# New places in the instruction order of all five engines, in a kernel of attention with a Hyena gate

## The chip, the cores and the metric

The kernel runs on one core of one Trainium2 chip. The metric is the device time of one execution in microseconds (us); it is given as the median of several runs. A core has five instruction queues that matter here: PE (TensorE, the matmuls), ACT (ScalarE), DVE (VectorE), POOL (GpSimd) and SP (SyncE, which here only issues DMA transfers). Each works through its own queue strictly in order.

## What is computed

For each of 8 batches, 12 heads attend over 448 positions of 64 values. The denominator of the softmax has one more term, as if there were one more key with score 0. The heads of a position side by side make the 768 columns of `x`, which goes through a projection, a convolution along the sequence (by Fourier transform, with one filter for each column), a gate and an output projection.

```python
scores = scale * np.matmul(q, k.transpose(0, 1, 3, 2))
m = np.max(scores, axis=-1, keepdims=True)
e = np.exp(scores - m)
attn = e / (np.sum(e, axis=-1, keepdims=True) + np.exp(-m) + 1e-09)
x = heads_side_by_side(np.matmul(attn, v))           # 8 x 448 x 768
proj = x @ w_proj                                    # 768 x 2304
x1, x2, x3 = proj[..., :D], proj[..., D:2*D], proj[..., 2*D:]
x2_conv = np.fft.irfft(np.fft.rfft(x2, n=S, axis=1) * H, n=S, axis=1)
y = x1 * x2_conv * x3
out = y @ w_out                                      # 768 x 768
```

## The kernel before

**Tiling.** Two heads make a pair; a batch has 6 pairs, the whole input 48, numbered `i` (pair 12 is the first of batch 2, the third batch). For each pair TensorE computes the transposed scores (`scores`, L835 to L842) in four tiles of keys, `t` = 0 to 3: three of 128 keys, and tile 0 with the last 64 keys of both heads. ScalarE takes the exponential (L844), TensorE multiplies with V, which has a column of ones for the denominator (`out_rests` L867, `out_rest` L876 with the matmul at L879), and VectorE normalises into `xb` (L887). Then `xb` is turned to `xT`, by TensorE or by a DMA transpose.

**How Q and K are turned.** Batches 0 and 1 are "staged" (`staged`, L449): SP loads q, k and v of a pair (the tasks `sq`, `sk`, `sv`; 224, 192 and 192 KB), POOL or VectorE casts them to bf16 (`cq`, `ck`, `cv`; casts of v at L505), and TensorE turns q and k (`T`). From batch 2 on (`loaded`, L592) POOL casts likewise, and then SP issues DMA transposes from `qn` to `qT` (L600) and from `kn` to `kT` (L607), one pair at first and three at a time later. The transpose of K of pair 12 (`kT12`) needs the cast `ck12`, the two casts `crk2` of the batch's last 64 keys (L621, from the load `rk2`) and the memset of `kn` (`zero kn`, L1507). The first scores of a pair, S(i,0), need its `kT` and `qT`.

**Dense part of a batch** (`dense`, L1012). The projection to x2 is done in the folded domain of the transform (`proj2`, L1065 to L1068, with weights `w(1,0)` and `w(1,1)`, or `still2` for later batches, with DMA transposes between), then the products with the filter's spectrum (`product`, L1154), the two gates (`gate`, L1187, with weights `w(0)` and `w(2)`), the inverse transform, the gating, and the projection by `w_out` (`output`, L1000), whose tiles ScalarE copies out and SP stores. The weights are loaded and cast to bf16 by DMAs that POOL issues: `filt`, `w(0)`, `w(1,0)`, `w(1,1)`, `w(2)` (`wproj_load`, L816 to L818) and `wout` (L822 to L823, 1152 KB in bf16). While batch b is in its dense part, the attention of batch b + 1 runs on the same engines; the instructions are interleaved.

**What sets the order.** The kernel's body doesn't write the instructions out in sequence. Each piece of work is handed to a planner as a task (`add`, L77): an engine, a cost, what it needs and makes, and which ring buffers it takes and gives back. There are 2027 tasks: 605 on PE, 549 on DVE, 453 on ACT, 243 on SP, 177 on POOL. The planner sorts each engine's tasks and plays the program through with the costs, to place tiles in PSUM banks and to put idle matmuls into gaps of the first 36 us. Where the list `ORDER` is set (L406), the k-th task's number in it is the key by which its engine's tasks are sorted, and the engine takes only the first of its queue:

```python
want = self.ORDER[len(self.tasks)] if self.ORDER else want + self.SHIFT.get(part, 0.0)
queue = {e: sorted(t for t in self.tasks if t[2] == e) for e in self.LAT}
for i, t in enumerate(queue[e][: 1 if self.ORDER else self.WINDOW]):
```

So an engine's instructions run in the order of these numbers, whatever the costs say, and an instruction that waits for data holds up all behind it on its engine. SP's queue holds loads, DMA transposes and stores in one sequence.

Of the kernel before, what the change touches and what calls it, by code (L numbers as in the profile page):

```python
# [300 lines left out]
def kernel(  # L301
# [92 lines left out]
    def stage(g, at, n):  # L394
# [4 lines left out]
    plan = Plan(  # L399
        {  # L400
            "e": 6, "er": 2, "k0": 2, "q0": 2, "u": 1, "w": 1, "xf": 1,
            "x2": 1, "x2s": 1, "x2h": 1, "xs": 2, "t0": 2, "t1": 2, "yh": 1, "g": 1, "x1": 2, "cr": 2, "cw": 1, "cv": 2, "yT": 1, "yR": 1,
            "os": 3,
        }
    )
# [1126 lines left out]
    with (  # L1532
# [6 lines left out]
        for b in range(n_batches):  # L1539
            W["yT", b], W["yR", b // 2] = y, yr  # L1540
            stable(b)
            plan = Plan(plan.size)
# [9 lines left out]
    with tc.manual_schedule(engines={E.PE, E.Pool, E.DVE, E.Activation, E.SP}):  # L1552
        plan = main
# [31 lines left out]
```

## Time and profile before

| | before |
|---|---|
| median of 3 runs | 376.19 us |
| lowest and highest run | 375.47, 376.73 us |
| span of the profiled execution | 375.5 us |
| ScalarE, VectorE, GpSimd busy | 264.3, 259.1, 114.7 us |
| TensorE busy | 361.1 us |

The profile is of one execution. A line of a table of groups gives engine, operation, tile and source line; in the timeline the first two numbers are the start and the duration, and a bracket at the end is the idle time just before with what ended it. SP's queue is shown as SPq and POOL's as POOLq. A DMA issue's line belongs to the helper that issues it: L601 for the transposes to `qT`, L608 for those to `kT`, L818 for `w`, L823 for `wout`. A transfer's "us to landing" runs from its issue to its last byte. A table of windows gives, for a stretch of time, each engine's busy time with the number of instructions, then the granted clock of TensorE (1.00 is full), the share of the DMA engines and GB/s.

### The profile page before, as it was taken

To read this page: it belongs to the slowest core of one execution; us is meant where nothing else is said; L and a number is where in the kernel's file an instruction comes from. 1 tells how busy PE (TensorE), PEld (TensorE's weight loads), DVE (VectorE), ACT (ScalarE), POOL (GpSimd) and SP (SyncE) were. 2 spreads that over 40 slices of the span, in tenths; PEclk is the share of its full clock that TensorE was granted. 3 is DMA by queue.
4 is the path that set the end of the run, shared out by engine and by line. 5 is a ranking of instruction groups with operands and counts; after the bars stand their busy time and mean duration, and the time that the engine had idled before them with its cause. 6 is when DMAs were issued, how large, how long until landed. Compare 5 with 4: busy or idle time off the path is not lost. (4 is left out here: it accounts for less than half of the span.)

```text
span 375.5 us, 9312 instructions
## 1 busy us (share of the span) xinstructions
PE 361.1 (96%) x3596; PEld 216.8 (58%) x3596; DVE 259.1 (69%) x676; ACT 264.3 (70%) x455; POOL 114.7 (31%) x240
## 2 busy tenths in 40 slices
PE   7999999799999999999899999999999999999995
PEld 6656665446755576655456556655555556555653
DVE  7589479845699657895299938685467855958770
ACT  4988976657886767788379568877788776536533
POOL 5862818024435363473264415330000000000000
PEclk9999999989999999999999999999999999999999
DMA  8999999999998999999999999787273026343214
GB/s 220 258 248 231 252 223 210 131 234 249 225 243 209 223 290 204 281 229 218 239 244 199 275 206 205 218 160 177 58 114 86 2 41 170 44 112 58 88 44 170
DMA packets 132018, 68.40 MB, mean 182 GB/s; under 512 B 88765, under 2 KB 128384, under 8 KB 131968
## 3 DMA queue, kind: packets, MB, share of 16 engines
q1 hardware_dynamic: 127248, 62.11, 73.5%
q0 software_dynamic: 4480, 5.41, 9.0%
q8 instruction: 29, 0.48, 0.5%
q10 hardware_dynamic: 240, 0.23, 0.2%
q14 instruction: 21, 0.17, 0.2%
HBM read 43.86 MB, written 11.01 MB: 146 GB/s over the span
## 5 line engine op out<-in xcount | busy, mean ns | idle before, releaser
L853 ACT ACTIVATE e<-psum 128x896 bf16<-128x896 f32 x144 | 126.8, 921 | 25.4 <-PE psum L840 21.2
L1190 PE MATMUL psum<-xT,wproj_bf 128*128 128x448 bf16 x576 | 122.1, 352 | 0.3 <-DVE ldm L1101 0.2
L1190 PEld LDWEIGHTS <-wproj_bf 128*128 128x128 bf16 x576 | 53.8, 97 | 46.1 <-issue 2.7
L1004 PE MATMUL psum<-wout_bf,yT 128*128 128x384 bf16 x288 | 53.9, 331 | 0.7 <-DVE g L1205 0.6
L879 PE MATMUL psum<-vn,e 128*128 128x65 bf16 x1152 | 47.5, 194 | 0.0
L879 PEld LDWEIGHTS <-e 128*128 128x128 bf16 x1152 | 41.6, 98 | 5.2 <-issue 0.8
L840 PE MATMUL psum<-qT,kT 64*128 64x448 bf16 x288 | 41.4, 357 | 0.3 <-ACT e L853 0.2
L637 POOL CAST nat<-nat 112x512 bf16<-112x512 f32 x36 | 26.0, 728 | 46.2 <-DMA nat<-in_q_dram 42.0
L1158 DVE TENSOR_TENSOR t<-xs,hrs 113x768 bf16<-113x768 bf16 (+1 forms) x64 | 37.3, 607 | 3.1 <-ACT xs L1152 2.7
L1004 PEld LDWEIGHTS <-yT 128*128 128x128 bf16 x288 | 27.3, 99 | 20.9 <-issue 3.9
L1090 PE MATMUL psum<-xf,wproj_bf 128*128 128x452 bf16 x180 | 38.8, 357 | 0.0
L1311 ACT COPY osb<-psum 128x384 f32<-128x384 f32 x56 | 25.7, 486 | 18.4 <-PE psum L1004 11.2
L859 ACT ACTIVATE er<-psum 128x448 bf16<-128x448 f32 x48 | 26.4, 552 | 17.1 <-PE psum L842 16.2
L1205 DVE TENSOR_TENSOR g<-x,psum 128x448 bf16<-128x448 bf16 x48 | 29.4, 615 | 12.2 <-PE psum L1190 8.5
L1152 ACT CAST xs<-psum 113x384 bf16<-113x384 f32 (+1 forms) x64 | 28.7, 486 | 9.5 <-PE psum L1140 5.7
L894 DVE TENSOR_TENSOR xb<-psum,den 128x512 bf16<-128x512 f32 x48 | 33.2, 691 | 1.7
L1245 ACT CAST cr<-psum 128x452 bf16<-128x452 f32 x48 | 24.7, 546 | 11.2 <-PE psum L1236 10.0
L1202 ACT CAST x<-psum 128x448 bf16<-128x448 f32 x48 | 25.6, 537 | 8.3 <-PE psum L1190 6.0
L892 DVE TENSOR_SCALAR den<-psum 128x8 f32<-128x8 f32 x48 | 7.9, 164 | 34.0 <-PE psum L879 32.7
L669 POOL CAST vn<-nat 128x192 bf16<-128x192 f32 x58 | 22.2, 409 | 21.4 <-DMA nat<-in_v_dram 16.9
L1068 PE MATMUL psum<-wproj_bf,xf 128*113 128x384 bf16 x144 | 27.0, 328 | 0.7 <-DMA wproj_bf<-in_moe_w_proj_dram 0.7
L657 POOL CAST nat<-nat 128x384 bf16<-128x384 f32 x29 | 18.0, 623 | 29.4 <-DMA nat<-in_k_dram 24.0
(128 smaller groups left out, 460.1 us busy)
## 6 DMA issues: line engine op xcount, KB each, us to landing
nat<-in_q_dram SPq DMA_DIRECT2D x47, 224.0 KB, 4.2
out_dram<-osb SPq DMA_DIRECT2D x24, 384.0 KB, 3.6
nat<-in_k_dram SPq DMA_DIRECT2D x41, 192.0 KB, 4.4
nat<-in_v_dram SPq DMA_DIRECT2D x41, 192.0 KB, 4.7
wproj_bf<-in_moe_w_proj_dram POOLq DMA_DIRECT2D x2, 1152.0 KB, 14.7
rests<-in_k_dram SPq DMA_DIRECT2D x8, 192.0 KB, 4.3
rests<-in_v_dram SPq DMA_DIRECT2D x8, 192.0 KB, 4.2
out_dram<-osb SPq DMA_DIRECT2D x8, 192.0 KB, 3.2
```

What stands on the lines that cost most here:

```text
L840: nc.tensor.matmul(sc[:, u, 0:S], kT[b % 2][c, hp, t, :], qT[b % 2][c, hp, :])
L853: nc.scalar.activation(to, of, AF.Exp, scale=SCALE)
L859: nc.scalar.activation(to, of, AF.Exp, scale=SCALE)
L879: nc.tensor.matmul(out_bank(u)[:, n, :], P["e"][1 + t][:, u * S + n * 128 : u * S + n * 128 + 128], vn[b % 2][:, hp, 4 * u + t, :], start= ...
L894: nc.vector.tensor_tensor(W["xb", b][:, hp].rearrange("p n (u d) -> p u n d", u=2), op[:, :, :, 0:DH], rec[:].unsqueeze(3).to_broadcast([1 ...
L1004: nc.tensor.matmul(ops[:n, :DCH], y[:, dt, 0:n], wout_bf[:, dt, ch * DCH : (ch + 1) * DCH], start=(dt == 0), stop=(dt == NDT - 1),)
L1068: nc.tensor.matmul(pps[:FQ, :DCH], W["xf", b][:, pg, kt, 0:FQ], wproj_bf[:, kt, D + ch * DCH : D + (ch + 1) * DCH], start=(kt == 0), stop= ...
L1090: nc.tensor.matmul(pps, wproj_bf[:, kt, D + dt * 128 : D + (dt + 1) * 128], W["xf", b][:, :, kt, 0:FQ], start=(kt == 0), stop=(kt == NDT - 1),
L1152: nc.scalar.copy(L["xs", par, ch][:K, pg % 2, :], L["Z", pg, ch][:K, :DCH])
L1158: nc.vector.tensor_tensor(t[:K], L["xs", par, ch][:K], h, op=ALU.mult)
L1190: nc.tensor.matmul(p[:, :S], wproj_bf[:, kt, 2 * part * D + dt * 128 : 2 * part * D + (dt + 1) * 128], xT()[:, kt, 0:S], start=(kt == 0), ...
L1205: nc.vector.tensor_tensor(g[:, dt, :], L["x1", dt], p[:, :S], op=ALU.mult)
```

## The change

One line differs, L406: the list `ORDER` has 2027 new numbers.

```diff
-    plan.ORDER = (17, 4, 0, 94, 7, 9, 8, 11, 21, 19, 26, 30, 5, 12, 200, 3, 6, 23, 2, 18, 13, 14,
+    plan.ORDER = (2, 2, 3, 171, 0, 3, 1, 0, 4, 1, 2, 3, 11, 1, 0, 0, 1, 6, 0, 5, 5, 9, 8, 7, 5,
...
```

Before, the numbers are one ranking of all tasks, from 0 to 2026; after, they count within each engine. Since only the order within an engine is read, what matters is a task's place in its engine's queue. No task, cost, tile, buffer or instruction is added or taken away. The place is the same as before for 186 of 605 tasks on PE, 156 of 453 on ACT, 91 of 549 on DVE, 34 of 243 on SP and 16 of 177 on POOL. A task moves by 1.6 places on PE, 1.3 on ACT, 3.0 on DVE, 4.4 on POOL and 4.6 on SP in the mean, and by at most 16 on PE, 46 on SP and 155 on POOL. The moves that matter below:

| queue | task | place before | place after |
|---|---|---|---|
| POOL | first DMA of 32 bytes (L1463; nobody waits for it) | 16 | 171 |
| POOL | `pads` (zeros in the exponentials' tiles) | 2 | 11 |
| POOL | `crv0` (cast of the last keys' V, batch 0) | 8 | 13 |
| POOL | load `filt` | 9 | 15 |
| POOL | loads `w(0)`, `w(1,0)` | 20, 21 | 21, 27 |
| POOL | load `w(1,1)` | 36 | 33 (behind `cv6`, ahead of `ck8`, `cq8`) |
| POOL | load `w(2)` | 38 | 38 |
| POOL | load `wout` | 54 | 42 (behind `cq10`, ahead of `cv7`, `ck11`, `cv8`, `cq11`) |
| POOL | casts `crk2`; `ck12` | 50, 55; 58 | 51, 53; 52 |
| SP | loads `sv7`, `sv8` | 24, 35 | 33, 36 |
| SP | loads `sq11`, `sk11` | 37, 38 | 34, 35 |
| SP | transposes `qT12`, `kT12` | 50, 52 | 46, 49 |
| SP | loads `sv13`, `sq15`; transpose `qT13` | 45, 49; 51 | 51, 56; 53 |
| SP | a store of batch 2 | 189 | 173 |
| SP | x2 transpose of batch 3; an xT transpose | 160; 103 | 152; 99 |
| DVE | memset `zero kn` | 74 | 91 |
| PE | S(12,0) | 131 | 131 |

In SP's queue after, the places 26 to 36 hold `sk8`, `sq8`, `sk9`, `sq9`, `sk10`, `sq10`, `sv9`, `sv7`, `sq11`, `sk11` and `sv8`, in this order. On PE, five output tiles of the last batch come in another sequence; their stores don't.

2 lines of the change are left out of this document (1 added, 1 removed).

## The prediction

> **What bounds the kernel now.** I read the page's head and clock row first, then the table of waits of TensorE, then the windows around its longest wait.
>
> ```profile
> span 375.5 us, 9312 instructions
> PE 361.1 (96%) x3596; PEld 216.8 (58%) x3596; DVE 259.1 (69%) x676; ACT 264.3 (70%) x455; POOL 114.7 (31%) x240
> PEclk9999999989999999999999999999999999999999
> ```
>
> TensorE is busy for 361.1 of 375.5 us, and the next engine for 264.3. So the time is TensorE's work plus what it waits for; an order can change only the second, some 14 us, and what the clock loses. The clock row has one 8, in its ninth slice (75 to 84 us). The profiled execution's span is 375.5 us and the median 376.19; I work on the span and add the 0.7 at the end.
>
> ```profile
> PE psum L842 <- DMA kT<-nat: 3.2, 1, 3.2
> PE psum L1480 <- DVE idle L1468: 2.0, 1, 2.0
> PE psum L1140 <- DMA x<-ldm: 0.8, 1, 0.8
> PE psum L1068 <- DMA wproj_bf<-in_moe_w_proj_dram: 0.7, 2, 0.5
> PE psum L842 <- DVE xT L985: 0.7, 1, 0.7
> ```
>
> The columns are the total, the count and the longest. The longest wait by far is at L842, the first scores of pair 12, for pair 12's DMA transpose of K. L1480 is the start of the program.
>
> ```profile
> 72.00:74.00 2.00, 0.76 (x5) 0.20 (x2) 2.00 (x6) 0.63 (x2) 0.00 (x0) 1.00 1.41 137
> 74.00:76.00 2.00, 0.06 (x1) 0.06 (x1) 0.55 (x2) 0.00 (x0) 0.00 (x0) 1.00 1.15 165
> 76.00:78.00 2.00, 2.00 (x39) 1.39 (x40) 0.12 (x1) 1.66 (x3) 0.80 (x2) 0.89 1.16 306
> 78.00:80.00 2.00, 2.00 (x8) 0.86 (x6) 1.87 (x6) 0.50 (x1) 0.92 (x3) 0.50 1.24 257
> 80.00:82.00 2.00, 2.00 (x12) 0.70 (x11) 1.77 (x5) 0.92 (x1) 0.00 (x0) 0.76 1.57 174
> ```
>
> After the length of the window come PE, PEld, DVE, ACT, POOL, then the granted clock, the DMA share and GB/s. TensorE all but stops from 72.8 to 75.9, and behind that the clock falls to 0.89, 0.50 and 0.76. TensorE is full there, so the loss is 0.22 + 1.00 + 0.48 = 1.7 us. One late transpose costs 3.2 + 1.7 = 4.9 us.
>
> Why it was late, from the timeline and the DMA issues (the first three from 60.2 to 66 us, the last two of the whole run; KB each, then us to landing):
>
> ```profile
> 60.32 0.82 POOL L823 DMA_DIRECT2D wout_bf<-in_moe_w_out_dram  x1
> ...
> 63.52 0.85 DVE L1158 TENSOR_TENSOR t<-xs,hrs 112x768 bf16<-112x768 bf16 x1
> 64.14 3.92 SPq L608 DMA_TRANSPOSE kT<-nat  x1
> 70.33 2.43 PE L1190 MATMUL psum<-xT,wproj_bf 128*128 128x448 bf16 x12
> 75.94 0.36 PE L842 MATMUL psum<-qT,kT 128*128 128x448 bf16 x1 [3.18 <-DMA kT<-nat]
> ```
>
> ```profile
> wout_bf<-in_moe_w_out_dram POOLq DMA_DIRECT2D x1, 1152.0 KB, 14.1
> qT<-nat SPq DMA_TRANSPOSE x2, 13.2
> kT<-nat SPq DMA_TRANSPOSE x1, 11.8
> ```
>
> ```profile
> qT<-nat SPq DMA_TRANSPOSE x16, 4.5
> kT<-nat SPq DMA_TRANSPOSE x16, 4.4
> ```
>
> The load of the output weights was issued at 60.32, the transposes right behind it, and they took 11.8 to 13.2 us where the median of the run is 4.4. The transpose of K was issued at 64.14, landed at 75.9, and was needed at 70.33 + 2.43 = 72.8.
>
> **The change part by part.** Nothing is added or removed: no instruction, tile or wait on a semaphore, only places in the queues. So each cost is a wait that goes or comes.
>
> *Output weights ahead (POOL place 54 to 42).* They are now issued right behind cq10 and w(2), some 10 us earlier, and are through when the transposes come.
>
> ```profile
> DMA packets 2330, 1.79 MB, mean 149 GB/s; under 512 B 1252, under 2 KB 2328, under 8 KB 2328
> q0 software_dynamic: 783, 1.18, 78.3%
> q1 hardware_dynamic: 1545, 0.59, 39.6%
> ```
>
> ```profile
> DMA packets 1420, 1.61 MB, mean 230 GB/s; under 512 B 45, under 2 KB 1419, under 8 KB 1419
> ...
> q1 hardware_dynamic: 694, 0.57, 31.6%
> ```
>
> The first fence is 62 to 74 us (q0 is GpSimd's queue, q1 SyncE's; packets, MB, share): load and transposes together moved 149 GB/s. The second is 24 to 31 us, a weight load beside plain loads: 230 GB/s. At about 226, the 1.79 MB of 62 to 74 take 7.9 us instead of 12: 4.1 earlier. In SyncE's queue sv13, sq15 and qT13 (0.42 MB) also move behind K's transpose: 0.42 / 0.23 = 1.8 us. The transpose then lands at 75.9 - 5.9 = 70.0.
>
> Its issue is gated too: it needs the memset of kn (L1507), which moves back from place 74 to 91 on VectorE, where the work stood at 63.52 (row above), and behind it on POOL two casts of the shared rows and ck12, 0.5 us each:
>
> ```profile
> 53.34 0.38 DVE L1507 MEMSET nat<- 128x384 uint32 x1
> 61.19 0.51 POOL L621 CAST nat<-rests 64x384 bf16<-64x384 f32 x1
> ```
>
> The memset thus ends at about 64.4 at the latest, the three casts at 65.9, the issue is at 66.2, and with the median 4.4 us it lands at 70.6. Both ways leave 2 us before 72.8. Wait **-3.2**, clock **-1.7**. Bounds: nothing gained at one end, -4.9 at the other; I take the far end because both estimates have slack.
>
> *w(1,1) ahead (POOL place 36 to 33: behind cv6, ahead of ck8 and cq8).*
>
> ```profile
> 34.04 0.64 POOL L505 CAST vn<-nat 128x192 bf16<-128x192 f32 x2 [1.06 <-DMA nat<-in_v_dram]
> 38.41 0.82 POOL L818 DMA_DIRECT2D wproj_bf<-in_moe_w_proj_dram  x1
> ```
>
> ```profile
> 48.70 1.18 PE L1068 MATMUL psum<-wproj_bf,xf 128*113 128x384 bf16 x6 [0.52 <-DMA wproj_bf<-in_moe_w_proj_dram]
> 54.16 0.93 PE L879 MATMUL psum<-vn,e 128*128 128x65 bf16 x24
> ```
>
> It was issued at 38.41 and is now issued at 34.7, when cv6 ends, so the 0.52 us at 48.70 goes: **-0.5**.
>
> *What it meets: V of pair 8.* The same load now runs beside SyncE's loads of pairs 8 to 11, and in SyncE's queue V of pair 8 stands at 36, behind sk8, sq8, sk9, sq9, sk10, sq10, sv9, sv7, sq11 and sk11. These and itself are 7 x 0.197 + 4 x 0.229 = 2.29 MB. Its cast cv8 releases the output matmuls of pair 8 (L879, at 54.16; TensorE would be there at 53.7 with the 0.5 gained). SyncE's rate, from 37 to 42 us without a weight load and from 43 to 48 and 49 to 55 with one, and last GpSimd's queue from 38 to 43:
>
> ```profile
> DMA packets 1611, 1.27 MB, mean 255 GB/s; under 512 B 98, under 2 KB 1611, under 8 KB 1611
> ```
>
> ```profile
> q0 software_dynamic: 774, 0.66, 81.6%
> q1 hardware_dynamic: 649, 0.48, 39.0%
> ```
>
> ```profile
> q1 hardware_dynamic: 1411, 0.46, 38.0%
> ```
>
> ```profile
> q0 software_dynamic: 106, 0.08, 10.4%
> ```
>
> Alone 255 GB/s; beside w(1,1) 0.48 MB in 5 us, 96 GB/s; beside w(2) 0.46 in 6 us, 77 (and by the fence of 24 to 31, 0.57 in 7, 81). By 36.4, when the load before it, w(1,0), is through, I count 0.16 MB of the 2.29 as done (an estimate, most of one transfer). From there: w(1,1)'s bytes start at about 38.7, 4 us behind its issue (issued at 38.41, its queue had moved only 0.08 MB by 43), 2.3 us at 255 = 0.59 MB; w(1,1) takes 0.59 MB / 0.132 = 4.4 us, 0.42 MB beside it; about 1.1 us until w(2) starts, 0.28 MB. There remain 0.84 MB beside w(2) at 81: 10.4 us, until 54.6. With the cast (0.64) cv8 is there at 55.3, against 53.7 to 54.2: a wait of 1.1 to 1.6. I take **+1.3**. Bounds: 0, if w(2) starts later; 7.9, worked out below.
>
> *The first 36 us* (filter 9 to 15, pads 2 to 11, crv0 8 to 13 on POOL). ScalarE sets the pace there:
>
> ```profile
> 10.00:20.00 10.00, 9.58 (x143) 6.24 (x143) 5.43 (x17) 9.65 (x15) 8.96 (x19) 1.00 1.14 252
> ```
>
> ScalarE is busy for 9.65 of 10 us, and its order hardly moves. I take 0, with the waits below 1 us of the table as bounds, about 2 either way.
>
> *After 85 us* SyncE's order (store(2,2) 189 to 173, some x transposes up to 8 places earlier) can move the waits of L1140 and L842: -1.5 (0.8 + 0.7) if both go, +4.9 if a transpose meets a load as in 64 to 76. I take 0: no weight load is left there, the first DMA (POOL 16 to 171) has nobody waiting for it, and TensorE's own moves (16 places at most) keep the work the same around each wait above. *Tail*: the last batch's output tiles are computed in another sequence and stored in the same one; 0 to +0.3, taken as 0.
>
> Sum: -3.2 - 1.7 - 0.5 + 1.3 = -4.1 us; span 371.4, and by the median 376.19 - 4.1 = **372.1 us**.
>
> **Rivals.**
>
> *V of pair 8 becomes the late transfer (slower).* Beside back-to-back weight loads SyncE moved only 0.59 MB in 12 us (49 GB/s) from 62 to 74. If it gets no more behind w(1,1), with w(2) and the output weights now following each other, the 0.84 MB take 17.1 us, to 61.3; cv8 comes at 62.0, a wait of 7.9, and a wait this long halves the clock too, 1.7. That is -5.4 + 7.9 + 1.7 = +4.2: 380.4. It decides from a wait of 3.7, which is 65 GB/s. For it: the three loads stand closer together than before. Against it: those 12 us held transposes, and without them SyncE had 77 to 96 beside a load. 0.15; 0.05 more for a like delay elsewhere.
>
> *K's transpose stays late.* The load may not have slowed it; then only the 1.8 us of moved items come off, it lands at 74.1, 1.3 are left of the wait, the clock stays full: -1.9 - 1.7 - 0.5 + 1.3 = -2.8, 373.4. Against it: 13.2 and 11.8 us beside the load, 4.4 in the median. 0.11. [...] The trace's 149 against 230 GB/s speaks against it.
>
> *Given back later.* A transpose or a store behind 85 us is delayed, 2.3 us of wait and 1.7 of clock: 376.1, no change. For it: SyncE's later places move most (46 at most). Against it: every wait there is below 1 us. 0.13.
>
> *All goes well.* V of pair 8 is in time (-1.3) and the 0.8 and 0.7 go as well: 369.3. 0.08.
>
> [...]
>
> **How the numbers follow.** The forecast (370.5 to 373.5) has 0.48, the others 0.15 + 0.05, 0.11, 0.13, 0.08. The range goes from the last rival to a V wait halfway into the first: 369.2 to 378.0. About 0.3%, 1.1 us, is what a measurement can tell from no change: faster 0.48 + 0.11 + 0.08 = 0.67, same 0.13, slower 0.20.
>
> **What would show it.** The output weights issued near 50; K's transpose of pair 12 landed in under 7 us, before 72; no L842 row of 3.2; no 8 in the clock row's ninth slice; no wait at L1068 at 48; a wait of about 1 us at L879 near 54 for pair 8's cast. Wrong if that wait is above 3.7 us, if K's transpose is still the late one, or if waits below 36 or beyond 85 us change by more than 1 us.

## The result, and the profile after

| | before | after |
|---|---|---|
| median of 20 runs each | 376.40 us | 379.31 us |
| lowest and highest | 372.74, 381.06 | 377.20, 382.30 |
| ratio, with 95% interval | | 1.0106 (1.0078 to 1.0133) |
| span of the profiled execution | 375.5 us | 377.0 us |

The changed kernel is slower, by 1.06% or 4.0 us. The ratio is taken from the executions in the faster of two states, which leaves out the dearest of the kernel before; over all 20 of each the medians differ by 2.9 us. Forecast was 372.1, and 379.31 lies above the range that was given (369.2 to 378.0). First the head of the page of the changed kernel:

```profile
span 377.0 us, 9293 instructions
PE 359.6 (95%) x3584; PEld 216.1 (57%) x3584; DVE 255.8 (68%) x676; ACT 263.4 (70%) x455; POOL 109.4 (29%) x240
PEclk9999999999999999999999999999999999999998
```

The 8 in the ninth slice is gone (the one in the last slice lies behind the last matmul). TensorE is busy for 359.6 instead of 361.1 us, nearly the 1.7 us that the clock cost (twelve idle matmuls fewer are in it too). So the part of the prediction that it was about came true, and yet the span is longer. TensorE's waits in the changed kernel (total, count, longest):

```profile
PE psum L1190 <- DMA wproj_bf<-in_moe_w_proj_dram: 1.5, 1, 1.5
PE psum L1140 <- DMA x<-nat: 1.4, 1, 1.4
PE psum L840 <- DVE xb L894: 1.4, 1, 1.4
PE psum L1068 <- DMA wproj_bf<-in_moe_w_proj_dram: 1.2, 1, 1.2
...
PE psum L840 <- DVE g L1205: 0.7, 1, 0.7
```

The row of L842 with its 3.2 us is gone. In its place stand rows of 0.7 to 1.5 us, at several places of the kernel; five of them are shown. From the timeline and the DMA issues (66 to 70 us) of the changed kernel, the chain that was mended:

```profile
42.89 0.82 POOL L823 DMA_DIRECT2D wout_bf<-in_moe_w_out_dram  x1
62.96 1.32 SPq L601 DMA_TRANSPOSE qT<-nat  x1
66.93 3.55 SPq L608 DMA_TRANSPOSE kT<-nat  x2
```

```profile
kT<-nat SPq DMA_TRANSPOSE x2, 3.3
```

Pair 12's transpose of K was issued at 66.93 (66.2 was predicted) and landed at 71.0, before TensorE needed it.

**Where the time goes.** The order of TensorE's work differs, so I compare by work done: for each point, the time at which TensorE had done so much, less the streaming time of that work at full clock (the same in every column, so it cancels in the differences). The growth of this number in a stretch is what TensorE lost there, waits and half clock together, in us. The times of the heads are those of the changed kernel. Two further profiles of the kernel before (e5 and e6, below) and two of the changed one with small edits (e4, e10) show how much of it is one execution's chance. The profile of e10 is of its dearest execution (379.43 us, the others 375.6 to 377.6):

| stretch | before: first, e5, e6 | after, e4, e10 | difference of the means |
|---|---|---|---|
| 2 to 71 us | 18.5, 18.2, 18.2 | 19.2, 20.5, 19.2 | +1.3 |
| 71 to 109 | 7.2, 4.8, 5.8 | 3.0, 2.2, 2.9 | -3.2 |
| 109 to 187 | 6.4, 6.1, 5.7 | 7.9, 7.0, 8.6 | +1.7 |
| 187 to 272 | 4.7, 4.6, 4.6 | 5.6, 6.1, 7.9 | +1.9 |
| 272 to 279 | 0.4, 0.4, 0.4 | 2.0, 1.1 (e10 mends it: 0.5) | +1.1 |
| 279 to 368 | 3.9, 3.9, 3.9 | 4.1, 4.1, 4.0 | +0.1 |
| last matmul to the end | 4.2 | 5.3 (e4 mends it: 4.2) | +1.1 |

The sum is +4.0 us, of which 0.2 go off because TensorE starts that much earlier; the measured ratio is 4.0 us. The stretch that the prediction was about gained 3.2 us; all the others lost 7.2.

**The end** is the plainest of them. The last issues on SyncE's queue, the changed kernel first and then the kernel before, each with the last store's KB and us to landing:

```profile
371.61 1.11 SPq L1321 DMA_DIRECT2D out_dram<-osb  x2
372.82 0.54 SPq L1318 DMA_DIRECT2D out_dram<-osb  x1
...
out_dram<-osb SPq DMA_DIRECT2D x1, 384.0 KB, 3.3
```

```profile
370.24 1.14 SPq L1321 DMA_DIRECT2D out_dram<-osb  x2
372.19 0.34 SPq L1318 DMA_DIRECT2D out_dram<-osb  x1
...
out_dram<-osb SPq DMA_DIRECT2D x1, 384.0 KB, 2.3
```

With the new sequence of tiles the issue of tile 3's two stores ends only 0.1 us ahead of the last store's, instead of 0.8. Beside them the last store took 3.3 instead of 2.3 us.

### The profile page after: what moved, and what is told of

The parts are those of the page before. It is cut to its first block, busy times and chain, and to the rows that moved or that the text cites. A ratio compares the mean times of both kernels' runs of the same rounds, so it can differ in the third digit from the quotient of the medians.

```text
span 377.0 us, 9293 instructions
## 1 busy us (share of the span) xinstructions
PE 359.6 (95%) x3584; PEld 216.1 (57%) x3584; DVE 255.8 (68%) x676; ACT 263.4 (70%) x455; POOL 109.4 (29%) x240
## 5 line engine op out<-in xcount | busy, mean ns | idle before, releaser
L1190 PEld LDWEIGHTS <-wproj_bf 128*128 128x128 bf16 x576 | 53.5, 97 | 47.2 <-issue 3.1
L1004 PE MATMUL psum<-wout_bf,yT 128*128 128x384 bf16 x288 | 52.9, 326 | 0.4 <-DVE g L1205 0.4
L879 PEld LDWEIGHTS <-e 128*128 128x128 bf16 x1152 | 42.8, 98 | 5.7 <-issue 0.8
L637 POOL CAST nat<-nat 112x512 bf16<-112x512 f32 x36 | 23.5, 655 | 72.2 <-DMA nat<-in_q_dram 38.0
L840 PE MATMUL psum<-qT,kT 64*128 64x448 bf16 x288 | 41.3, 355 | 2.5 <-DVE xb L894 1.4
L1158 DVE TENSOR_TENSOR t<-xs,hrs 113x768 bf16<-113x768 bf16 (+1 forms) x64 | 36.4, 592 | 3.1 <-ACT xs L1152 3.0
L1068 PE MATMUL psum<-wproj_bf,xf 128*113 128x384 bf16 x144 | 26.4, 328 | 1.2 <-DMA wproj_bf<-in_moe_w_proj_dram 1.2
L669 POOL CAST vn<-nat 128x192 bf16<-128x192 f32 x58 | 21.1, 394 | 20.0 <-DMA nat<-in_v_dram 18.9
L1090 PEld LDWEIGHTS <-wproj_bf 128*128 128x128 bf16 x180 | 16.4, 96 | 16.8 <-issue 1.5
```

The source lines that it names most:

```text
L840: nc.tensor.matmul(sc[:, u, 0:S], kT[b % 2][c, hp, t, :], qT[b % 2][c, hp, :])
L879: nc.tensor.matmul(out_bank(u)[:, n, :], P["e"][1 + t][:, u * S + n * 128 : u * S + n * 128 + 128], vn[b % 2][:, hp, 4 * u + t, :], start= ...
L1004: nc.tensor.matmul(ops[:n, :DCH], y[:, dt, 0:n], wout_bf[:, dt, ch * DCH : (ch + 1) * DCH], start=(dt == 0), stop=(dt == NDT - 1),)
L1068: nc.tensor.matmul(pps[:FQ, :DCH], W["xf", b][:, pg, kt, 0:FQ], wproj_bf[:, kt, D + ch * DCH : D + (ch + 1) * DCH], start=(kt == 0), stop= ...
L1090: nc.tensor.matmul(pps, wproj_bf[:, kt, D + dt * 128 : D + (dt + 1) * 128], W["xf", b][:, :, kt, 0:FQ], start=(kt == 0), stop=(kt == NDT - 1),
L1158: nc.vector.tensor_tensor(t[:K], L["xs", par, ch][:K], h, op=ALU.mult)
```

## The experiments

**Halves and single moves (e1 to e4).** Theory: the early part of the new order gains, the late part gives back. The rivals said that the gain was chance, or that the loss was early. All four ran on one chip against the same runs of before (375.59 us).

```diff
 e1, POOL's queue of before, one load moved:
   ... cq10,
+  wout,
   ck10, cv11, cv9, cv8, cv10, cq11, ck11, crk2, crv2, cq13, cq12,
-  wout,
   crk2, cv13, ck14, ck12 ...
 e2: all five queues new for what starts before 85 us, then before's order
 e3: before's order for what starts before 85 us, then the new one
 e4, the changed kernel, TensorE's last tiles as in before:
-  (3,1) (2,0) (1,1) (3,0) (2,1)
+  (1,1) (3,0) (3,1) (2,1) (2,0)
```

> Before's order with one task moved: the output weights' load goes from place 54 to 42 of POOL's queue, as in the changed kernel. Theory (the wait of pair 12 for its transpose of K costs 4.9 us in every execution, and the load is its cause): that wait and the half clock behind it go, ratio to before 0.987 to 0.990. Rival 1 (the load is the cause, but the profiled execution of before had an unusually long wait, and the typical one loses less): the profile shows the early load and no wait, ratio 0.994 to 1.000. Rival 2 (the load isn't the cause, or its new place delays SyncE's loads as much): a wait of over 2 us at pair 8 or 12 in the profile, ratio 1.000 or above.

> All engines in the new order for what starts in the first 85 us, in before's order from there. Theory (the new order gains early and gives it back late): by the profiles TensorE is 4.0 to 4.4 us ahead of before at 85 us, ratio 0.988 to 0.991. Rival 1 (the early gain is a matter of the one profiled execution of before): 0.996 to 1.002. Rival 2 (the loss is early, in the waits for the weights at 33 and 38 us): 1.004 or above.

> All engines in before's order for what starts in the first 85 us, in the new order from there. Theory (the loss is late: by the profiles 4.8 us of new waits between 90 us and the last matmul and 0.9 in the last stores): ratio 1.012 to 1.016. Rival 1 (the late waits are chance, the loss is early): 0.998 to 1.002. Rival 2 (part of the late loss only follows from TensorE being early, so that it isn't there when the early part is late): 1.003 to 1.008.

> The changed kernel, with the last batch's output tiles and their copies in before's sequence. Theory (with the new sequence two stores of tile 3 are issued right ahead of the last store, which then takes 4.2 instead of 3.3 us to land): 0.9 us less than the changed kernel, ratio to before 1.007 to 1.009. Rival (the end's difference between the two profiles is chance): as the changed kernel, 1.0106, within its interval of 1.008 to 1.013.

| run | median | ratio to before | 95% interval |
|---|---|---|---|
| e1, the load alone | 377.70 us | 1.0067 | 1.0029 to 1.0105 |
| e2, early part new | 379.01 | 1.0094 | 1.0059 to 1.0128 |
| e3, late part new | 379.90 | 1.0137 | 1.0072 to 1.0203 |
| e4, new with old tail | 378.31 | 1.0066 | 1.0030 to 1.0102 |

e3 is as the theory had it: the late part of the new order costs 1.4% by itself. e4 is in its direction, 0.4% below the changed kernel (the intervals overlap; that the end is mended is read from its trace, 4.2 us from the last matmul as in before). e1 and e2 refute the theory's other half: both take away the wait at pair 12 and are slower than before (e1 has the ratio of its second rival without its wait). In e1 only one load is moved. Its DMA queues from 50 to 60 us, and below them those of e5 (the kernel before) in the same stretch; q0 is GpSimd's weight loads, q1 SyncE's transfers:

```profile
q0 software_dynamic: 1074, 1.61, 87.9%
q1 hardware_dynamic: 1393, 0.48, 27.1%
```

```profile
q1 hardware_dynamic: 3266, 1.66, 89.9%
q0 software_dynamic: 410, 0.61, 33.1%
```

SyncE's queue moved 0.48 MB in these 10 us instead of 1.66 (the changed kernel: 0.53). The delay didn't go; it moved from pair 12's transposes to the loads of pairs 12 to 15: in e1 the Q load of pair 12 landed at 63.96 instead of 59.51. GpSimd's casts of these loads came later with it, and met other work of VectorE. VectorE in e1, with what it ran beside on GpSimd, and then e5:

```profile
69.29 0.38 DVE L1256 TENSOR_TENSOR cw<-cr 128x444 bf16<-128x444 bf16 x1
69.59 0.88 DVE L1254 TENSOR_TENSOR cw<-cr 128x452 bf16<-128x452 bf16 x1
70.50 1.31 DVE L1265 TENSOR_TENSOR cv<-cw 128x448 bf16<-128x448 bf16 x2
```

```profile
69.55 0.61 POOL L637 CAST nat<-nat 112x512 bf16<-112x512 f32 x1 [2.56 <-DMA nat<-in_q_dram]
70.11 0.85 POOL L669 CAST vn<-nat 128x192 bf16<-128x192 f32 x2
70.91 0.66 POOL L657 CAST nat<-nat 128x384 bf16<-128x384 f32 x1
```

```profile
69.65 0.39 DVE L1256 TENSOR_TENSOR cw<-cr 128x444 bf16<-128x444 bf16 x1
69.95 0.40 DVE L1254 TENSOR_TENSOR cw<-cr 128x452 bf16<-128x452 bf16 x1
70.38 0.69 DVE L1265 TENSOR_TENSOR cv<-cw 128x448 bf16<-128x448 bf16 x2
```

The same three instructions take 0.88 and 1.31 us beside the casts and 0.40 and 0.69 without them. TensorE, 2.7 us earlier here than in e5, then waited for VectorE three times from 76 to 87 us (0.2 to 0.4 us each) and twice at 107 and 110 (0.4 and 0.7). Behind 110 us 0.4 of the 2.7 us are left; behind a further wait at 152 us (0.9, at L1236) e1 is 1.7 us later than e5. That the casts slow VectorE and that this is what costs TensorE its lead is read from the traces; no run tried it by itself.

e3, whose late waits are the ones in question:

```profile
PE psum L1140 <- DMA x<-ldm: 1.6, 1, 1.6
...
PE psum L1140 <- DMA x<-nat: 0.9, 1, 0.9
```

The first stands at 181.6 us, and behind it the granted clock is at half for 3.4 us (183.3 to 186.7), 1.7 us more. From 109 to 187 us e3 lost 3.5 us more than the mean of before, from 187 to 272 only 0.4: the loss is late as in the changed kernel, but not at the same places. Nor do the halves add up: e2 costs 0.94% and e3 1.37%, the whole order 1.06%. So the table above says where the time went, not what each part of the order would cost alone.

**The kernel before again, and the load put back (e5 to e7).**

> The kernel before, unchanged, profiled again. Theory (its executions are of two kinds: in one pair 12's transpose of K is late enough that the clock halves, mean granted clock 0.991 to 0.995; in the other the clock stays at 0.998 to 1.000 and the time is some 2.9 us less): with a clock of 0.998 or more the wait at L842 near 75 us is below 2 us and no slice of the clock row shows 8, and the time is 373.5 to 376; with a clock of 0.995 or less, as in the profile known. Rival (the clock's dip is elsewhere): the wait is 3 us in both kinds.

> As the run ahead of it: a third profile of the kernel before, for the same question.

e7 is the changed kernel with the load of the output weights behind cq13 instead of cq10.

> The changed kernel with the output weights' load back behind the casts of pairs 12 and 13 (place 55 of POOL's queue, 54 before). Theory (in this order the early load is what keeps pair 12's transposes in time): the transposes of pair 12 take over 8 us again, a wait of 1 to 3 us at L842 near 72 us, often with the clock down; ratio to before 1.011 to 1.018. Rival (the new places of SyncE's loads and transposes alone do that, and the early load costs time elsewhere, as it did alone): ratio 1.002 to 1.008.

e5 took 374.28 us, e6 374.82. Their rows of L842 and their clock rows, e5 first:

```profile
PE psum L842 <- DMA kT<-nat: 2.5, 1, 2.5
```

```profile
PEclk9999999999999999999999999999999999999999
```

```profile
PE psum L842 <- DMA kT<-nat: 1.8, 1, 1.8
```

```profile
PEclk9999999989999999999999999999999999999999
```

With the first profile: a wait of 3.2 us and a dip, one of 2.5 and none, one of 1.8 and a dip. So the wait is there in all three and varies; the theory's "below 2 us without a dip" is wrong in its number, and the dip doesn't follow from the length of the wait alone. Of the 26 runs of before that the comparison of e1 to e4 used, 10 had a mean granted clock of 0.991 to 0.995 and took 377.1 us in the mean, 16 had 0.998 to 1.000 and took 374.8. The execution on which the prediction was worked out was one of the dearer ones.

e7: 382.99 us, ratio 1.0210 (1.0159 to 1.0260), above what the theory had, and not by the way that it had. Pair 12's transposes were in time without the early load (Q's took 3.1 us, K's 5.0, landed at 71.5), and TensorE had no wait for them. GpSimd had waited 6.7 us, until 65.0, for the memset of `kn`, which the new order has later on VectorE, so the load behind these casts was issued at 67.45 instead of 60.32 and landed at 77.8, and TensorE waited for the weights themselves:

```profile
PE psum L1004 <- DMA wout_bf<-in_moe_w_out_dram: 2.6, 1, 2.6
```

So with all else new the early load is needed, but for its own use and not for pair 12.

**The price of the transfer, and other ways to take away the wait (e8 to e11).**

In these lists `X36` is SyncE's transpose of x of pairs 36 to 38 (`X18`: 18 to 20), `x2(5, ...)` a transpose of x2 of batch 5, and `G4` a group of gate matmuls.

```diff
 e8:
-        nc.gpsimd.dma_start(wout_bf, moe_w_out.rearrange("(t p) c -> p t c", p=128))
+        nc.gpsimd.dma_start(wout_bf[:, 0], moe_w_out[0:128, :])
...
-                wout_bf[:, dt, ch * DCH : (ch + 1) * DCH],
+                wout_bf[:, 0, ch * DCH : (ch + 1) * DCH],
 e9, before's order:
   POOL: ... cq12, wout, crk2,
+  ck12,
   cv13, ck14,
-  ck12,
   cq15 ...
   SP: ... sq15, qT12,
-  qT13, kT12,
+  kT12, qT13,
   sk16 ...
 e10, e4 and, on SP:
-  X36, x2(5, second half),
+  x2(5, second half), X36,
 e11, e10 and: POOL's filt from place 15 to 10, w(1,0) from 27 to 22, PE's first G4 from 59 to 64
```

> The kernel before, but only the first sixth (192 KB) of the output weights is loaded, and every output matmul uses this sixth: the instructions are the same, the output isn't the reference's. It prices the transfer itself. Theory (the other 960 KB, running beside SyncE's transfers from 60 to 74 us, are the cause of pair 12's late transpose, and moving them to 42 us only moved the delay to the loads of pairs 12 to 15): no wait at L842 near 74 us, transposes of 4 to 6 us, and no later loads either, ratio to before 0.986 to 0.993. Rival 1 (the transpose is late for its place in the queues): a wait of over 1.5 us stays, ratio 0.997 to 1.002. Rival 2 (VectorE paces the stage from 60 to 110 us, so that TensorE gives back what it gains): no wait at L842, but new waits for VectorE at 76 to 110 us of 2 us or more, ratio 0.995 to 1.002.

> The kernel before with two tasks moved: the cast ck12 on POOL from place 58 to 56, right behind the second cast of the shared keys, and on SyncE the transpose of Q of pair 13 behind pair 12's of K (place 51 to 52). The output weights stay where they are. Theory (pair 12's transpose of K need only be issued some 2 us earlier): its issue moves from 64.3 to about 62.5, it lands 2 to 3 us earlier, the wait at L842 falls from 2.0 to 3.4 to below 0.7 us, and since no load of pairs 12 to 15 comes later nothing is given back: ratio 0.992 to 0.996. Rival 1 (it lands when the output weights let it, whenever it is issued): wait unchanged, 0.998 to 1.002. Rival 2 (given back behind it, as with the output weights moved): 1.000 to 1.007.

> The changed kernel with before's sequence of the last output tiles (as in the run e4) and, on SyncE, the second x2 transpose of batch 5 ahead of the transpose of x of pair 36 (places 222 and 221 exchanged, which is before's order of the two). Theory (the 0.7 to 1.6 us of wait at L1140 near 272 to 279 us in all profiles with the new late order come from that transpose's place): the wait falls below 0.5 us, ratio to before 1.002 to 1.005, against 1.0066 for e4. Rival (the loads of pairs 45 to 47, which the new order issues 20 us later than before, delay it whatever its place): the wait stays, ratio 1.005 to 1.009.

> As e10, and the first weights as early as in before: on POOL the filter's load from place 15 to 10, w(1,0) right behind w(0), and on TensorE the first gate matmuls (G4) five places later. Theory (the early loss of about 1 us is TensorE's wait for w(0) and w(1,0), 1.5 and 1.2 us at 33 and 38 us): both waits below 0.6 us, ratio to before 0.998 to 1.003, about 0.3% below e10. Rival (earlier weights delay SyncE's loads of pairs 6 to 8 as much): new waits for casts at 25 to 45 us, ratio as e10 or above.

| run | median | ratio to before | 95% interval |
|---|---|---|---|
| e8, a sixth of the output weights | 372.75 us | 0.9943 | 0.9890 to 0.9996 |
| e9, pair 12's K issued earlier | 374.87 | 0.9976 | 0.9925 to 1.0026 |
| e10, old tail and x2 earlier | 377.01 | 1.0032 | 0.9986 to 1.0078 |
| e11, and first weights earlier | 378.82 | 1.0094 | 1.0041 to 1.0146 |

e8: the load is the cause. Issued at 64.53, at the same place as before, the transpose of K took 4.9 us instead of 10.5 (e5) and landed at 69.4; TensorE had no wait for it. But even with 960 KB less to move the gain is 0.6%, 2.1 us in the mean, not 4.9. The six executions fall into two groups: four took 372.6 to 372.8 us with a mean clock of 0.998 to 1.000, two 375.8 and 376.7 with 0.994. The profile is of the dearest. It shows a wait that isn't in the kernel before, and VectorE's reason for it:

```profile
PE psum L1236 <- DVE g L1205: 2.3, 1, 2.3
```

```profile
148.07 0.17 DVE L1037 COPY xT<-xT 128x6 bf16<-128x6 bf16 x1 [4.02 <-DMA xT<-xb]
```

At 144 us VectorE's queue comes to the first use of batch 3's transposed x (pairs 18 to 20), waits 4.0 us for SyncE's transpose, which landed at 148.05, and the gating product that TensorE waits for stands behind it. Behind TensorE's wait the granted clock was 0.52 and 0.62 from 152 to 156 us, 1.7 us more. These 4.0 us are about what sets this execution apart from the four cheap ones; whether those have the wait too isn't known, as none of them was profiled. In e5 this transpose landed at 146.0, and TensorE was late enough not to wait. In e9 it landed at 146.0 too, while TensorE was 1.0 us further: the same wait, 1.1 us. By these profiles SyncE's queue, with its loads, transposes and stores, is a second pace beside TensorE's, and who is ahead of it waits.

In e9's profile K's transpose was issued at 61.9 instead of 64.3 and landed at 72.7 instead of 74.8 (e5), and the wait was 0.7 us. That this came of the earlier issue isn't shown. e12 (below) has the same order up to 140 us; there the transpose was issued at 62.0 and landed at 74.8, with the old wait and a dip of the clock behind it:

```profile
PE psum L842 <- DMA kT<-nat: 2.4, 1, 2.4
```

What all seven profiles with the output weights' load in its old place share (the first, e3, e5, e6, e9, e12, e13) is another thing: the transpose, issued at 61.9 to 64.5, landed 0.7 to 1.5 us behind the last byte of that load, which came at 72.0 to 74.5. That is e9's first rival, that it lands when the output weights let it, and e9's ratio can't be told from no change.

e10 confirms one late term: with the second x2 transpose of batch 5 ahead of x of pair 36 TensorE loses 0.5 us instead of 1.1 to 2.0 from 272 to 279 us (a wait of 0.7 us for the batch's first x2 transpose stands just ahead of that stretch). Four of the loads of pairs 45 to 47 were issued at 235 to 240 us before; the new order issues them at 256 to 267, among these transposes. The ratio fits the theory (its interval also reaches e4's). e11 goes to its rival: TensorE no longer waits for w(0) and w(1,0), but it waits 1.6 us at L533 for casts of K (0.9 in e10) and was no earlier at 71 us.

**Whether the give-back can be moved away (e12 to e15).**

```diff
 e12 = e9, e13 = before, e14 = e1, each with, on SP:
   kT27, sv27,
+  X18,
   kT24, sv29,
-  X18,
   sq27 ...
 e15 = e10 with, on DVE: the normalisation of pair 23 ahead of xf, cw, cw, xf, cv (five places),
   the product g of batch 3 ahead of cv, cv, y, xf (four places)
```

> As e9 (ck12 and pair 12's transpose of K earlier, the output weights where they were), and on SyncE the transpose of x of pairs 18 to 20 two places earlier, ahead of pair 24's transpose of K. Theory (in e1, e8 and e9 TensorE gave its gain back at 151 us, because VectorE waits there in order for that transpose, and what TensorE waits for stands behind it): the transpose lands 2 to 3 us earlier, at 142 to 144, VectorE's wait at L1037 near 146 falls below 0.7 us, TensorE's wait at L1236 near 151 goes, ratio to before 0.990 to 0.996. Rival (the gain is given back at the next place): ratio as e9, 0.996 to 1.000.

> The kernel before with only the second move of e12: the transpose of x of pairs 18 to 20 two places earlier. Theory (behind the long wait for pair 12 TensorE is late enough that VectorE's wait for this transpose is covered): no change, 0.998 to 1.001. Rival (an earlier transpose is worth about 1 us whatever came before): 0.995 to 0.998.

> As e1 (before with the output weights' load at place 42), and the transpose of x of pairs 18 to 20 two places earlier. Theory (part of e1's loss is the wait at 152 us for that transpose, 1.0 us, the rest the loads of pairs 12 to 15 that come 4 us later, with waits at 76 to 110 us): ratio 1.003 to 1.005 against e1's 1.0067. Rival 1 (nearly all of it is that wait): 0.997 to 1.002. Rival 2 (the wait only moves on): 1.006 or above.

> As e10 (the changed kernel with before's last tiles and the x2 transpose of batch 5 ahead of x of pair 36), and on VectorE two tasks earlier: the normalisation of pair 23 four places, and the gating product that TensorE waits for at 207 us four places, ahead of the two unfolding sums of 0.4 us that take 0.7 to 1.8 us each there beside GpSimd's casts. Theory (these sums, slowed by the casts, stand ahead of what frees a PSUM bank for TensorE): the waits at L840 near 162 and 208 us (0.9 to 1.8 in the profiles of the new order) fall below 0.5 us, ratio 0.998 to 1.002 against e10's 1.0032. Rival (VectorE is late there altogether, so that the wait only moves): as e10, 1.002 to 1.005.

| run | median | ratio to before | 95% interval |
|---|---|---|---|
| e12 | 376.86 us | 1.0023 | 0.9983 to 1.0063 |
| e13 | 375.92 | 1.0016 | 0.9978 to 1.0053 |
| e14 | 378.32 | 1.0090 | 1.0056 to 1.0123 |
| e15 | 377.14 | 1.0060 | 1.0021 to 1.0098 |

None gained anything that can be measured. In e14 and e15 the wait that was aimed at is gone and another is there. In e14 no wait is left at 152 us, but this row is new, at 224; in e15 none of 0.5 us or more at L840 near 162 and 208, but this one is new, at 182 (e14 first):

```profile
PE psum L840 <- DVE ldm L1101: 2.5, 2, 2.3
```

```profile
PE psum L1090 <- DVE ldm L1101: 1.6, 1, 1.6
```

So the rivals "the wait only moves on" have it for both by their times; with one profile each it isn't shown that the new wait comes of the move. The transpose did land earlier in e13 and e14 (143.7 and 144.7 us, against 146.0 in e5 and 147.5 in e1). In e12 it landed at 145.8, no earlier than in e9, but this profile is of one of its dearest executions (379.24 us, mean clock 0.990); against my theory e12's time is not below e9's. e13 is no change, as expected. No version that gives the reference's output beats the kernel before clearly; e9 is the nearest, and isn't told apart from it.

## Why the prediction was wrong, step by step

- **"Wait -3.2, clock -1.7."** Right in the cause (e8) and in what the changed kernel does: issue near 43 (predicted 50), K's transpose in 4.1 us, no row of L842, no dip. Wrong in size: 4.9 us was one execution's, and the stretch from 71 to 109 us gained 3.2 against the mean of three. The working for the landing counted 1.79 MB from 62 to 74 us, though 1.18 of them are the load that moves away; this did no harm, since the issue, not the rate, set the landing.
- **"The wait at L1068 near 48: -0.5."** It went. But w(1,1) was issued at 37.07, not 34.7: cv6, ahead of it, waited for a load that landed at 36.4, as I hadn't checked.
- **"V of pair 8: +1.3."** It didn't come; the load landed at 49.3, not 54.6. The rate beside a load was too high all the same: I took 77 to 96 GB/s, and from 50 to 60 us SyncE had 53 in the changed kernel and 48 in e1, the 49 GB/s of my slower rival. I put its price at the wrong transfers. The loads of pairs 12 to 15 pay it. The sum also has no loss of clock behind these 1.3 us; no run shows that at pair 8, but behind the waits of 1.2 to 1.5 us that the changed kernel had elsewhere (they end at 32.7, 37.8, 162.2 and 275.9 us) the granted clock was 1.00.
- **"The first 36 us: 0, about 2 either way."** Up to 71 us the new order lost 1.3: new waits for w(0) and w(1,0), 1.5 and 1.2 us. Inside the bounds, but on the wrong side, and e11 shows that it isn't mended by moving those loads.
- **"After 85 us: I take 0."** This is the step that failed. From 109 us to the last matmul the new order lost 4.8 us (1.7 + 1.9 + 1.1 + 0.1), and e3, with the new order only for what starts behind 85 us, lost 5.1 by itself (2.7 to 7.6, the stores at the end included). I had reasoned that no weight load is left there. But up to 46 places of movement on SyncE's queue, and 3.0 in the mean on VectorE's, need no weight load to do harm. The rival "given back later" had the direction; I gave it 0.13 and one place of 4.0 us, where there were several of 1 to 2. The last sign that I had named for being wrong, waits beyond 85 us that change by more than 1 us, is the one that came. e4 and e10 show what the end and the stretch from 272 to 279 us lost; which moves cost the 3.6 us from 109 to 272 stays open.
- **"Tail: 0 to +0.3."** +1.1, the last store issued 0.2 us later behind its copy and landing 1.0 us later.

Behind all of these is one assumption: that a wait taken away from TensorE is time gained. e1 and e2 took away the wait at pair 12 and were 2.5 and 3.5 us slower for it. e8 took it away too and gained 2.1 us in the mean, and its profile of a dear execution shows 4.0 us given back at one later place.

The wait at 208 us shows a second thing that the prediction didn't price. L1265 on VectorE in the changed kernel (ns: least, middle, longest of 48), with the timeline around the longest:

```profile
L1265 DVE TENSOR_TENSOR cv<-cw x48: 374/385/1823, 68.6 to 364.6; 128x448 bf16<-128x448 bf16 x48
```

```profile
203.10 0.72 POOL L621 CAST nat<-rests 64x384 bf16<-64x384 f32 x1 [0.68 <-DMA rests<-in_k_dram]
203.50 2.32 DVE L1265 TENSOR_TENSOR cv<-cw 128x448 bf16<-128x448 bf16 x2
203.78 0.66 POOL L657 CAST nat<-nat 128x384 bf16<-128x384 f32 x1
204.39 0.63 POOL L669 CAST vn<-nat 128x192 bf16<-128x192 f32 x2
204.97 0.61 POOL L637 CAST nat<-nat 112x512 bf16<-112x512 f32 x1
205.64 0.55 POOL L621 CAST nat<-rests 64x384 bf16<-64x384 f32 x1
...
207.08 0.60 DVE L1205 TENSOR_TENSOR g<-x,psum 128x448 bf16<-128x448 bf16 x1
207.74 0.36 PE L840 MATMUL psum<-qT,kT 64*128 64x448 bf16 x2 [0.71 <-DVE g L1205]
```

An addition that takes 0.385 us in the middle of 48 took 1.82 us, 4.7 times as long, while GpSimd's casts followed each other with hardly a gap. The product that TensorE waited for stands three instructions behind. Around the same time the kernel before has its casts in runs of three or four with gaps between, and its longest addition took 0.83 us in the first profile and 1.25 in e5. That the casts do it wasn't tried by itself; it is read from the traces, which don't show in what way they would.

Transposes were not the only transfers that were slow. In e1, beside the weight load, plain loads were as slow as the transposes had been: Q's two loads that were issued at 42.6 and 52.0 us took 15.9 us in the mean, where e5 has 11.0 and the transposes of pair 12 had 10.5 to 13.2. By these traces what is slowed is SyncE's whole queue, and the separation of transposes from weight loads only chose another victim.

## What to carry to other kernels

A wait on the engine that bounds the kernel needn't be worth its length (without the one at pair 12 e1 was 2.5 us slower than before, e8 2.1 us faster): look first at who else is nearly as late there (an in-order neighbour that waits for a DMA queue, a queue that is never empty), for that is where the wait can stand next. A transfer moved ahead can take its bandwidth from other transfers (in e1 SyncE's queue moved 0.48 MB in 10 us instead of 1.66); name them, and what is released by them. And when a whole order is laid anew, price the places where nothing seems to happen, and profile the kernel before more than once: here its main wait was 1.8, 2.5 and 3.2 us in three executions. The same holds for a run that confirms: e9's profile looked like a success, and e12's, with the same order up to that place, did not.

## What the runs showed of the hardware

- Beside weight loads of GpSimd's queue SyncE's queue got 48 to 53 GB/s in three stretches: 0.53 MB in 10 us with plain loads issued (after, 50 to 60 us), 0.48 in 10 with loads and one transpose (e1, 50 to 60), 0.59 in 12 with loads and transposes (before, 62 to 74). In three others of the kernel before, 24 to 31, 43 to 48 and 49 to 55 us, it got 77 to 96.
- With a load of 1152 KB on GpSimd's queue, a transpose of SyncE's queue issued at 61.9 to 64.5 us landed 0.7 to 1.5 us behind the load's last byte in seven profiles of seven.
- A VectorE addition of two tiles of SBUF (128x448, bf16) took 1.82 us instead of 0.385 beside an unbroken run of GpSimd casts, in the changed kernel from 203.5 us; that these are the cause wasn't tried by itself.
- A wait of 1.8 us was followed by a dip of the granted clock in one execution (e6), and one of 2.5 us by none in another (e5); of two waits of 2.3 us one had a dip behind it (e8) and one had none (e14).
